# Windowed attention and a gated FFN on one core: the first fp32r term of each split unit's keys rounded on ScalarE and not on VectorE

## The chip, the cores and the metric

The kernel runs on one core of one Trainium2 chip. The metric is the device time of the whole program in microseconds (us). Three runs of the kernel before took 1072.38, 1073.99 and 1076.33 us, median 1073.99. One further execution, 1072.04 us, was profiled; all rows shown are from it.

## The reference

Sliding-window attention (each query sees itself and the 127 keys before it, with a linear bias per head), then a two-layer FFN with a sigmoid-gated unit on the attention's output, 4608 tokens of 512 features, all in float32:

```python
scores = scale * np.matmul(q, k.transpose(0, 1, 3, 2))       # q, k, v: (8, 8, 576, 64)
mask = (rel >= 0) & (rel < 128)                               # rel = query - key
scores = np.where(mask, scores + bias[None], -1000000000.0)
attn = np.exp(scores - np.max(scores, axis=-1, keepdims=True))
attn = attn / (np.sum(attn, axis=-1, keepdims=True) + 1e-09)
attn_out = np.matmul(attn, v)
x = attn_out.transpose(0, 2, 1, 3).reshape(4608, 512)
h = x @ w_in                                                  # 512 -> 2048
g = h * (1.0 / (1.0 + np.exp(-1.702 * h)))
return g @ w_out                                              # 2048 -> 512
```

## The kernel before

TensorE multiplies in fp32r, a float32 format with fewer mantissa bits. To keep float32 accuracy a number a is held as two fp32r terms: the first is a rounded, the second is a minus the first. A product then takes two or three matmuls.

The work has three parts in time. From the start to about 195 us attention of the first two batches runs in "whole" units, beside loads and the decoding of the weights. From about 195 to 765 us attention of batches 2 to 7 runs in 120 "split" units, woven into the FFN's steps. From 765 us to the end only the FFN is left, in a form that reuses precomputed combinations of the weights. The change touches only the middle part.

A split unit is one or two blocks of 128 queries of one pair of heads. Its steps, each a function of the kernel, go through the engines like this:

- `load`: queries `rq` and keys `rk` come by DMA on SP's queue. A unit has 256 or 128 queries (two blocks or one and a half, as columns) and 384 or 256 keys.
- `split_q` (L308): ScalarE copies `rq` into `Q`, the first term of the queries.
- `split_rest` (L326 to L328): VectorE copies `rk` into `K1`, the first term of the keys. GpSimd then subtracts to make the lower half of `Q` the second term (L327), and subtracts `K1` from `rk` to make `K2` (L328).
- `scores` (L350): TensorE multiplies `Q` with `K1` and `K2` into the PSUM tile `s_ps`.
- `biased` (L378): VectorE adds bias to `s_ps`, writes `pb` and its minimum `mins`.
- `exponents` (L397): ScalarE takes the exponential of `pb` with `mins` as its bias.
- `normal` (L408, L409, L422): VectorE makes the reciprocal of the sums and scales `pb` by it.
- `flip`, `high`, `low` (L458, L471, L477): TensorE transposes `pb` into `t_ps`; ScalarE rounds it to `ph`; VectorE subtracts to get `pl`.
- `mix` (L515) and `sum_up` (L545 to L554): TensorE multiplies with the values `VV`; ScalarE, GpSimd and VectorE add the halves into `xf`, the FFN's input.

Each call of `tick` issues these steps for several units at once: the keys and queries of unit n+1, the scores of unit n, the softmax of unit n-1, the transposes of n-2, the mix of n-3. `K1`, `K2` and `Q` have two buffers each, so `K1` of unit n+1 may be written only when the scores of unit n-1, which read the same buffer, are done.

Beside it an FFN step f runs 12 matmuls of 128x256 into `h_ps` (L577), then tanh on ScalarE (L582), the gate on VectorE (L583), the rounding `gh` on ScalarE (L586), the second term `gl` on GpSimd (L587), and 6 matmuls of 128x512 into `acc` (L597). `h_ps` has two buffers.

What sets the order within each engine is a scheduler that runs over the whole program when it is built: it plays the program through with durations of its own and writes each engine's instructions in the order that comes out. Each engine then executes its list strictly in order. A step that moves to another engine can so change the order on all engines.

Of the kernel before, what the change touches and what calls it, by code (L numbers as in the profile page):

```python
# [153 lines left out]
def tile_kernel(ctx: ExitStack, tc: tile.TileContext, q0, k0, v0, qT, kT, v, w_in, w_out, out):  # L154
    nc = tc.nc
# [164 lines left out]
    def split_rest(u):  # L320
        if u.whole:
            return
        u.K1 = att.tile([P, 3 * P], F32R, name="K1")
        u.K2 = att.tile([P, 3 * P], F32R, name="K2")
        Q, K1, K2, rq, rk = u.Q[:, :u.nq], u.K1[:, :u.nk], u.K2[:, :u.nk], u.rq[:, :u.nq], u.rk[:, :u.nk]
        nc.vector.tensor_copy(K1, rk)  # L326
        nc.gpsimd.tensor_tensor(Q[D:], rq[D:], Q[D:].bitcast(F32), ALU.subtract)  # L327
        nc.gpsimd.tensor_tensor(K2, rk, K1.bitcast(F32), ALU.subtract)  # L328

# [486 lines left out]
    def tick():  # L816

        nonlocal ticks
        n = ticks

        def stage(k, *steps):
            u = units[n + k] if 0 <= n + k < len(units) else None
            for step in steps:
                if u:
                    step(u)

        stage(1, split_q)
        stage(-2, flip, split_v)
        stage(0, load_v)
        stage(-1, biased)  # L830
        stage(1, split_rest)
        stage(-1, exponents)
        stage(-1, normal)
        stage(-2, high, low)
        stage(0, scores)
        stage(-3, mix)
        if n + 1 < len(units) and units[n + 1] and loads:
            load(loads.pop(0))
        for ct in full.get(n - 3, ()):
            if ct > seen + 1:  # L840
                send(ct)
        ticks += 1
# [29 lines left out]
    fetch_upto(1)  # L872
    split_q(units[0])
    split_rest(units[0])
    while ticks < due[0][0] + 3:
        tick()
# [161 lines left out]
```

## Time and profile before

| | us |
|---|---|
| median of three runs | 1073.99 |
| profiled execution, its own time | 1072.04 |
| its span, first to last instruction | 1070.3 |
| TensorE busy | 1041.9 (97%) |
| VectorE (DVE) busy | 756.6 (71%) |
| ScalarE (ACT) busy | 631.9 (59%) |
| GpSimd (POOL) busy | 625.9 (58%) |

The profiled execution's own time is 1.95 us below the median of the runs, and 1.7 us longer than its span. PE is TensorE's matmuls, PEld its weight loads, which overlap the matmuls. Ends of matmuls are modelled, so a busy PE is not proof that it does its work at its peak rate. In rows of instructions, "K<-rk" means that a tile K (K1 or K2; numbers are left out) is written from rk, and the figures behind the bar are the group's busy time in us and the mean duration of one in ns, then the idle time of the engine just before them. In rows of waits the figures are the total in us, the number of times and the longest. Timeline rows begin with the start and the duration in us; a bracket at the end is the engine's idle time before.

### The profile page before, as it was taken

The page shows a single profiled execution, that of the slowest core. Times are in us where ns is not written, and L with a number is a line of the kernel's source. Part 1 is how long each engine was busy: PE and PEld are TensorE (multiplying, and loading weights), DVE is VectorE, ACT ScalarE, POOL GpSimd, SP SyncE. Part 2 cuts the span into 40 slices and gives each one's busy share as a digit, 9 for nine tenths or more (in the row PEclk, how much of TensorE's full clock was granted, in tenths as well). Part 3 has the DMA queues.
Part 4 walks back from the last instruction along what each step waited for, and adds up shares of the span by engine and source line. Part 5 has one row for each costly group of instructions (what it writes and reads, how often), then busy time and mean ns, then how long its engine had stood idle before and what let it go on. Part 6 is the DMA issues. An engine that isn't in the chain of part 4 may idle for free.

```text
span 1070.3 us, 21638 instructions
## 1 busy us (share of the span) xinstructions
PE 1041.9 (97%) x6897; PEld 913.5 (85%) x6897; DVE 756.6 (71%) x2184; ACT 631.9 (59%) x1854; POOL 625.9 (58%) x831
## 2 busy tenths in 40 slices
PE   9979999999999999999999999999999999999998
PEld 5667877788989989899898989999898998998987
DVE  6896676379888897988888798888854345436343
ACT  6968775466766766566666756667543344335332
POOL 4677986367776776667677667767642233215121
PEclk9989999999999999999999999999999999999999
DMA  8983446223234224324323332342165456545541
GB/s 306 386 300 129 142 154 194 87 83 90 80 87 133 77 83 130 109 82 125 99 77 104 118 108 79 89 138 78 59 228 191 173 177 210 177 165 202 192 177 60
DMA packets 120274, 151.90 MB, mean 142 GB/s; under 512 B 40032, under 2 KB 96864, under 8 KB 120160
## 3 DMA queue, kind: packets, MB, share of 16 engines
q1 hardware_dynamic: 114400, 140.55, 41.1%
q10 hardware_dynamic: 5760, 9.96, 2.5%
q8 instruction: 55, 0.90, 0.3%
q14 instruction: 59, 0.48, 0.1%
HBM read 119.01 MB, written 31.46 MB: 141 GB/s over the span
## 4 chain that ended last, share of the span: by engine, by line
PE 68%; DVE 11%; ACT 3%; issue 3%; POOL 1%; DMA 1%; POOLq 0%; ACTq 0%; SPq 0%; DVEq 0%
PE acc L597 17%; PE h_ps L577 17%; PE accs L777 11%; PE X_ps L718 6%; PE Y_ps L718 4%; PE x_ps L515 4%; PE s_ps L350 4%; PE t_ps L458 3%; DVE pb L422 2%; ACT pb L397 1%; PE x_ps L492 1%; DVE K L326 1%; DVE pb L378 1%; DVE pl L477 1%; DVE xl L563 1%
## 5 line engine op out<-in xcount | busy, mean ns | idle before, releaser
L577 PE MATMUL h_ps<-xh,w 128*128 128x256 f32 x1536 | 256.8, 289 | 7.8 <-DVE g L583 6.6
L577 PEld LDWEIGHTS h_ps<-xh,w 128*128 128x128 f32 x1536 | 217.8, 190 | 28.4 <-issue 7.3
L597 PE MATMUL acc<-w,gh 128*128 128x512 f32 x768 | 222.6, 402 | 0.4
L587 POOL TENSOR_TENSOR gl<-g,gh 128x256 fp32r<-128x256 f32 x192 | 149.4, 779 | 113.6 <-ACT gh L586 81.9
L730 POOL TENSOR_TENSOR gs<-g,gs 128x512 fp32r<-128x512 f32 x48 | 63.5, 1322 | 169.9 <-PE Y_ps L718 120.4
L777 PE MATMUL accs<-w,gs 128*128 128x512 f32 x576 | 148.4, 393 | 0.3 <-POOL gs L730 0.3
L397 ACT ACTIVATE pb<-pb,mins 128x256 f32<-128x256 f32 (+2 forms) x216 | 104.9, 486 | 73.3 <-DVE mins L378 71.7
L597 PEld LDWEIGHTS acc<-w,gh 128*128 128x128 f32 x768 | 130.8, 189 | 18.3 <-ACT gh L586 1.0
L328 POOL TENSOR_TENSOR K<-rk,K 128x384 fp32r<-128x384 f32 (+1 forms) x120 | 108.9, 908 | 51.6 <-POOL Q L327 10.4
L577 PE MATMUL h_ps<-xl,w 128*128 128x256 f32 x768 | 134.5, 283 | 0.0
L597 PE MATMUL acc<-w,gl 128*128 128x512 f32 x384 | 128.0, 407 | 2.2 <-POOL gl L587 2.2
L586 ACT CAST gh<-g 128x256 fp32r<-128x256 f32 x192 | 77.2, 404 | 79.7 <-DVE g L583 74.4
L777 PEld LDWEIGHTS accs<-w,gs 128*128 128x128 f32 x576 | 102.2, 189 | 17.7 <-POOL gs L730 0.7
L577 PEld LDWEIGHTS h_ps<-xl,w 128*128 128x128 f32 x768 | 111.5, 189 | 4.1 <-issue 0.4
L422 DVE TENSOR_SCALAR pb<-pb,rec 128x256 f32<-128x256 f32 (+2 forms) x216 | 109.1, 541 | 3.3
L583 DVE SCALAR_TENSOR_TENSOR g<-g,h_ps 128x256 f32<-128x256 f32 x192 | 78.9, 412 | 39.4 <-ACT g L582 38.2
L582 ACT ACTIVATE g<-h_ps 128x256 f32<-128x256 f32 x192 | 72.7, 380 | 40.2 <-PE h_ps L577 29.7
L327 POOL TENSOR_TENSOR Q<-rq,Q 64x256 fp32r<-64x256 f32 (+1 forms) x120 | 83.5, 696 | 18.7 <-DVE pb L422 1.9
L378 DVE CUSTOM_DVE_ANT_0 pb<-s_ps,bias 128x256 f32<-128x256 f32 (+3 forms) x240 | 85.4, 376 | 1.2
L458 PE MATMUL t_ps<-ident,pb 128*128 128x128 f32 x408 | 80.6, 274 | 4.6 <-DVE pb L422 2.9
L408 DVE TENSOR_SCALAR rec<-sums 128x2 f32<-128x2 f32 (+3 forms) x144 | 43.8, 304 | 53.2 <-ACT pb L397 46.2
L477 DVE TENSOR_TENSOR pl<-t_ps,ph 128x512 fp32r<-128x512 f32 (+2 forms) x120 | 72.0, 601 | 3.2 <-ACT ph L471 3.0
(114 smaller groups left out, 2064.6 us busy)
## 6 DMA issues: line engine op xcount, KB each, us to landing
ring<-part SPq DMA_DIRECT2D x84, 512.0 KB, 3.2
rk<-kT SPq DMA_DIRECT2D x72, 192.0 KB, 2.5
rq<-qT SPq DMA_DIRECT2D x96, 128.0 KB, 2.2
out<-o ACTq DMA_DIRECT2D x34, 256.0 KB, 2.7
rw<-w_in SPq DMA_DIRECT2D x16, 512.0 KB, 6.6
rw<-w_out SPq DMA_DIRECT2D x16, 512.0 KB, 7.0
x<-xf SPq DMA_DIRECT2D x13, 512.0 KB, 3.2
xf<-x SPq DMA_DIRECT2D x13, 512.0 KB, 4.3
```

The source lines that it names most:

```text
L327: nc.gpsimd.tensor_tensor(Q[D:], rq[D:], Q[D:].bitcast(F32), ALU.subtract)
L328: nc.gpsimd.tensor_tensor(K2, rk, K1.bitcast(F32), ALU.subtract)
L378: nc.vector.tensor_tensor_reduce(b.p[ra:rb, cs:b.end], u.s[ra:rb, e, cs:b.end], bias[head][ra:rb, cs:b.end], -SCALE, BIG, ALU.add, ALU.min ...
L397: nc.scalar.activation(live, live, AF.Exp, bias=u.mins[:b.rows, e:e + 1], scale=-1.0, accum_out=u.sums[:b.rows, e:e + 1],)
L422: nc.vector.tensor_scalar(live, live, u.rec[:rows, e:e + 1], None, ALU.mult)
L458: nc.tensor.transpose(u.t[:c.n, w:w + b.rows], b.p[:b.rows, col:col + c.n], ident[:b.rows, :b.rows])
L477: nc.vector.tensor_tensor(u.pl[:m, a:z], u.t[:m, a:z], u.ph[:m, a:z].bitcast(F32), ALU.subtract)
L577: nc.tensor.matmul(h, w1[f][:, z, k * P:(k + 1) * P], x[:, k], start=(n == 0), stop=(n == len(ops) - 1))
L587: nc.gpsimd.tensor_tensor(gl, g, gh.bitcast(F32), ALU.subtract)
L597: products.append(nc.tensor.matmul(acc, g[:, t * P:(t + 1) * P], w2[f][:, z], start=(f == self.f0 and n == 0), stop=(f == self.f1 - 1 and ...
L718: nc.tensor.matmul(bank, w[:, z, k * P:(k + 1) * P], x[:, y, k], start=start and i == 0, stop=i == len(ops) - 1, skip_group_check=True)
L777: products.append(nc.tensor.matmul(self.acc[t], g[:, y, t * P:(t + 1) * P], w2[f][:, z], start=(f == 0 and n == 0), stop=(f == NF - 1 and ...
```

## The change

The copy that makes `K1` is issued to ScalarE and not to VectorE. It is the same copy, of the same shapes, 120 times.

```diff
         Q, K1, K2, rq, rk = u.Q[:, :u.nq], u.K1[:, :u.nk], u.K2[:, :u.nk], u.rq[:, :u.nq], u.rk[:, :u.nk]
-        nc.vector.tensor_copy(K1, rk)
+        nc.scalar.copy(K1, rk)
         nc.gpsimd.tensor_tensor(Q[D:], rq[D:], Q[D:].bitcast(F32), ALU.subtract)
         nc.gpsimd.tensor_tensor(K2, rk, K1.bitcast(F32), ALU.subtract)
```

The scheduler then writes other orders from the first split unit on. Up to there all engines' lists are the same, and the last part of the FFN differs only at its join with the middle part. Numbers at names tell the buffers' instances apart. In the following rows K1_6302, Q_6285 and the scores s_ps_6236 belong to the same ticks: s_ps_6236 reads the buffer (then called K1_6122) that K1_6302 writes next. Rows of L378 are called ISA here and CUSTOM_DVE_ANT_0 in the profile.

VectorE around this unit, before:

```order
L554 TENSOR_TENSOR xf_4797<-x_ps_6140,xb_6243 64x128
L326 CAST K1_6302<-rk_6075 128x384
L378 ISA pb_6298,mins_6297<-s_ps_6236,bias0_76 128x256
L378 ISA mins_6297 128x1
L378 ISA pb_6300,mins_6297<-s_ps_6236,bias0_76 128x256
L378 ISA mins_6297 128x1
L408 TENSOR_SCALAR rec_6310<-sums_6307 128x2
```

and VectorE at the same place now:

```order
L583 SCALAR_TENSOR_TENSOR g_6190<-g_6190,h_ps_6177 128x256
L477 TENSOR_TENSOR pl_6207<-t_ps_6205,ph_6206 128x384
L378 ISA pb_6298,mins_6297<-s_ps_6236,bias0_76 128x256
L378 ISA mins_6297 128x1
L378 ISA pb_6300,mins_6297<-s_ps_6236,bias0_76 128x256
L378 ISA mins_6297 128x1
L408 TENSOR_SCALAR rec_6310<-sums_6307 128x2
```

The cast stood directly ahead of the minima of the scores (it does so in 109 of the 120 units), and they now follow the subtractions of an earlier unit.

ScalarE around the same unit, before:

```order
L315 CAST VV_6292<-rv_6117 128x2x64
L582 ACTIVATE g_6272<-h_ps_6259 128x256
L586 CAST gh_6275<-g_6272 128x256
L308 CAST Q_6285<-rq_6074 128x256
L397 ACTIVATE pb_6298,sums_6307<-pb_6298,mins_6297 128x256
L397 ACTIVATE pb_6300,sums_6307<-pb_6300,mins_6297 128x256
```

and ScalarE now:

```order
L586 CAST gh_6193<-g_6190 128x256
L326 CAST K1_6302<-rk_6075 128x384
L308 CAST Q_6285<-rq_6074 128x256
L545 COPY xb_6243<-x_ps_6140 64x512
L315 CAST VV_6292<-rv_6117 128x2x64
L397 ACTIVATE pb_6298,sums_6307<-pb_6298,mins_6297 128x256
L397 ACTIVATE pb_6300,sums_6307<-pb_6300,mins_6297 128x256
L582 ACTIVATE g_6272<-h_ps_6259 128x256
L586 CAST gh_6275<-g_6272 128x256
```

The cast now stands directly ahead of Q's (so in 104 of the 120 units), the exponentials follow behind both, and here the tanh and the rounding of one FFN step have moved from ahead of them to behind them.

TensorE where this unit's pb is transposed, before:

```order
L597 MATMUL acc1_6019<-w2_5_776,gl_6276 128x512
L577 MATMUL h_ps_6416<-xh_5906,w1_7_957 128x256 x5
L577 MATMUL h_ps_6416<-xl_5907,w1_7_957 128x256 x4
L577 MATMUL h_ps_6496<-xh_5906,w1_8_1045 128x256
L458 MATMUL t_ps_6368<-ident_75,pb_6298 128x128 x2
L458 MATMUL t_ps_6368<-ident_75,pb_6300 128x128
L597 MATMUL acc0_6018<-w2_6_874,gh_6356 128x512
```

and TensorE now:

```order
L577 MATMUL h_ps_6416<-xh_5906,w1_7_957 128x256 x4
L458 MATMUL t_ps_6368<-ident_75,pb_6298 128x128 x2
L597 MATMUL acc0_6018<-w2_5_776,gh_6275 128x512
L597 MATMUL acc1_6019<-w2_5_776,gh_6275 128x512
L597 MATMUL acc0_6018<-w2_5_776,gh_6275 128x512
L597 MATMUL acc1_6019<-w2_5_776,gh_6275 128x512
L458 MATMUL t_ps_6368<-ident_75,pb_6300 128x128
```

The transposes of pb_6298 stand earlier among the matmuls of FFN step 7, and four matmuls of step 5, which stood ahead of both, now stand between them and the transpose of pb_6300. TensorE's instructions are the same in number and shape.

## The prediction

> **What bounds the kernel now.** I read the page first, for the engines' shares and how they lie over time.
>
> ```profile
> span 1070.3 us, 21638 instructions
> PE 1041.9 (97%) x6897; PEld 913.5 (85%) x6897; DVE 756.6 (71%) x2184; ACT 631.9 (59%) x1854; POOL 625.9 (58%) x831
> DVE  6896676379888897988888798888854345436343
> ACT  6968775466766766566666756667543344335332
> ```
>
> TensorE is busy for 97% of the span, so it is the bound as a whole. DVE runs at eight to nine tenths in the middle slices, ACT at five to seven tenths. The next view was the busy time in three stretches: ahead of the split units, with them, behind them. After the stretch's length stand PE, PEld, DVE, ACT and POOL, each with its count.
>
> ```profile
> 0.00:195.00 195.00, 181.07 (x1151) 136.23 (x1152) 141.61 (x372) 143.60 (x428) 137.90 (x138) 0.97 0.67 225
> 195.00:765.00 570.00, 561.72 (x3882) 509.17 (x3881) 476.79 (x1588) 368.05 (x1159) 394.60 (x612) 1.00 0.33 97
> 765.00:1070.30 305.30, 299.10 (x1868) 268.11 (x1866) 138.24 (x225) 120.24 (x269) 93.40 (x82) 1.00 0.50 172
> ```
>
> Only the middle stretch holds the changed casts. There PE is busy for 561.72 of 570 us: 8.28 us of idle time is all that the rows offer to be won. DVE stands at 476.79/570 = 84%, ACT at 368.05/570 = 65%. So the question is not how much work moves, but whom TensorE waits for. The waits in this stretch, first PE's, then those of its weight loads, answer that:
>
> ```profile
> PE t_ps L458 <- DVE pb L422: 2.9, 5, 1.2
> PE s_ps L350 <- DVE mins L378: 1.8, 2, 1.2
> PE t_ps L458 <- DVE pl L477: 1.5, 1, 1.5
> PE acc L597 <- POOL gl L587: 1.2, 1, 1.2
> PE h_ps L577 <- DVE xh L561: 0.4, 1, 0.4
> PE x_ps L515 <- DVE xf L554: 0.2, 1, 0.2
> ```
>
> ```profile
> PEld t_ps L458 <- DVE pb L422: 4.2, 7, 1.4
> PEld acc L597 <- POOL gl L587: 1.6, 1, 1.6
> PEld acc L597 <- ACT gh L586: 0.7, 2, 0.3
> PEld x_ps L492 <- ACT pw L443: 0.3, 1, 0.3
> PEld x_ps L515 <- ACT ph L471: 0.2, 1, 0.2
> PEld x_ps L515 <- ACT g L582: 0.2, 1, 0.2
> ```
>
> PE's own waits come to 8.0 us, and 6.8 of them (2.9 + 1.8 + 1.5 + 0.4 + 0.2) end with a DVE instruction. ACT ends none of PE's and 1.4 us of the weight loads'. The scaled pb that comes too late for its transposes is the largest: 4.2 us in 7 waits by the weight loads' row. Each number is small: 0.5% of the median, about what a measurement of this kernel can tell from no change, is 5.4 us.
>
> **The work that moves.** The groups, with shapes kept apart:
>
> ```profile
> L326 DVE CAST K<-rk 128x384 fp32r<-128x384 f32 x72 | 34.3, 477 | 6.9 <-PE s_ps L350 4.3 <-issue 1.9 <-PE t_ps L435 0.2
> L326 DVE CAST K<-rk 128x256 fp32r<-128x256 f32 x48 | 18.8, 391 | 3.7 <-PE t_ps L435 2.1 <-PE s_ps L350 1.3
> L308 ACT CAST Q<-rq 128x256 fp32r<-128x256 f32 x96 | 38.9, 405 | 14.4 <-PE s_ps L350 10.3 <-issue 1.9 <-POOL VV L316 1.1
> L729 ACT CAST gs<-g 128x512 fp32r<-128x512 f32 x48 | 29.9, 623 | 18.9 <-DVE g L725 18.9
> ```
>
> DVE loses 34.3 + 18.8 = 53.1 us, 0.443 a unit: from 84% to 423.7/570 = 74%. On ACT the same copy of 256 columns takes 405 ns (Q's cast); 384 columns have no row, and half way between 405 and 623 is 514 ns. ACT so gains 48 x 0.405 + 72 x 0.514 = 56.4 us, 0.470 a unit: from 65% to 424.5/570 = 74%. The two engines come out level, and neither becomes the fullest: that stays PE. The edit issues no DMA of its own; on ACT's queue the casts now stand ahead of some issues of `out<-o`, which nothing in the middle waits for, and on SP's queue the scheduler only changed places among loads, which no PE row waits for.
>
> What a cast really occupied on DVE depends on its neighbour. The group's least, median and greatest duration, then two casts in the timeline, with what GpSimd did:
>
> ```profile
> L326 DVE CAST K<-rk x120: 275/353/1000, 202.5 to 763.9; 128x384 fp32r<-128x384 f32 x72, 128x256 fp32r<-128x256 f32 x48
> ```
>
> ```profile
> 401.64 0.74 POOL L587 TENSOR_TENSOR gl<-g,gh 128x256 fp32r<-128x256 f32 x1
> 401.98 0.62 DVE L326 CAST K<-rk 128x384 fp32r<-128x384 f32 x1
> 402.52 0.41 DVE L378 CUSTOM_DVE_ANT_0 pb<-s_ps,bias 128x256 f32<-128x256 f32 x1
> 402.97 0.51 ACT L397 ACTIVATE pb<-pb,mins 128x256 f32<-128x256 f32 x1 [1.17 <-DVE mins L378]
> ...
> 410.85 0.29 DVE L326 CAST K<-rk 128x256 fp32r<-128x256 f32 x1 [0.40 <-PE s_ps L350]
> 411.28 0.74 POOL L328 TENSOR_TENSOR K<-rk,K 128x256 fp32r<-128x256 f32 x1 [0.60 <-PE s_ps L350]
> ```
>
> The cast at 401.98 began while GpSimd worked on gl and ended at 402.60, after gl's end at 402.38; the narrower one at 410.85, with GpSimd idle, took 0.29. So part of the 53.1 us is waiting beside GpSimd. Q's cast on ACT has a mean of 405 ns for 256 columns, whatever GpSimd does.
>
> Here a rule speaks against the change. The Trainium skill, Perfetto Trace Analysis, section Optimizing Scalar/DVE Operations, says that where an operation has a VectorE performance mode VectorE is the faster engine, and that work is worth moving to ScalarE if VectorE is saturated. The trace agrees in direction for an undisturbed cast (0.29 against 0.405 us) but hardly for the means (391 against 405 ns). By that rule, with DVE unsaturated at 84%, the move would cost the difference, 56.4 - 53.1 = 3.3 us if all of it lay on the path, and give 1073.99 + 3.3 = 1077.3.
>
> **Where it stood and where it stands.** In the order of before the cast stands directly ahead of the minima in 109 of 120 units: DVE does K1, then the minima that ScalarE's exponentials need. The rows above show one such chain: cast, minimum at 402.52, exponential at 402.97 after 1.17 us in which ACT idled. Now the cast stands on ACT ahead of Q's cast. The waits of ACT, DVE and POOL in the stretch:
>
> ```profile
> ACT pb L397 <- DVE mins L378: 70.6, 80, 3.1
> ACT Q L308 <- PE s_ps L350: 12.4, 22, 1.2
> DVE rec L408 <- ACT pb L397: 45.1, 70, 1.5
> DVE g L583 <- ACT g L582: 15.7, 18, 5.1
> DVE K L326 <- PE s_ps L350: 5.6, 11, 1.0
> POOL K L328 <- DVE K L326: 4.2, 4, 1.8
> ```
>
> ACT idles ahead of an exponential 80 times, 70.6/80 = 0.88 us on average. That is the hole into which 0.47 us of cast falls. The minima come 0.44 us sooner; ACT is free 0.88 - 0.47 = 0.41 us sooner than the minima came before. So in these 80 units the exponentials start about 0.41 us earlier, although ACT does more. In the other 40 there was no hole, and ACT's queue is 0.47 us longer at most.
>
> **The sum, on the profiled execution's 1072.04 us.**
> 1. Transposes that wait for pb (4.2 us, 7 times): 7 x 0.41 = 2.9 us less, at best; by DVE's lighter load alone, 53.1/476.8 = 11% of 4.2, it is 0.5. I take -2.0, nearer the first, since the cast stood in that very chain.
> 2. Scores that wait for the minima to free s_ps (1.8 us, twice): 2 x 0.44 = 0.9 at best, 0.2 at least. I take -0.7.
> 3. pl and the DVE rest (1.5 + 0.4 + 0.2 us, three waits): between 0.2 and 3 x 0.44 = 1.3. I take -0.3, near the low end, since they stand behind other DVE work.
> 4. ACT's longer queue: in the 40 units without a hole pb comes 0.47 later. Now 7 of 120 transposes wait, so 40 x 7/120 x 0.47 = 1.1; by load alone 56.4/368 = 15% of the 1.4 us of weight loads that ACT ends, 0.2. I take +0.8. The ceiling, all 40 on the path, is 18.8.
> 5. The cast's own wait for the scores before last (DVE 5.6 us, 11 times): it goes to ACT, where Q's cast already waits for the same event (12.4 us, 22 times), and now ends ahead of Q's. No new wait, 0. K2 on GpSimd follows K1 as before; it waited 4.2 us for it and no row of PE waits for K2, since the scores that need it come a tick later: 0 between 0 and 4.2. If that cover were gone, the scores would be late next.
> 6. The orders that the scheduler rewrote: TensorE has the same instructions, and all that can change is its waits. From none left to twice as many, that is -8.3 to +8.3. I take 0, with +-3 for the range: a third of the idle time.
> 7. The stretches ahead and behind (195 + 305.3 us): same work, same order but for the join: 0.
>
> Sum: -2.0 - 0.7 - 0.3 + 0.8 = -2.2, so 1069.8 for a run like the profiled one. The median of the runs was 1.95 us above it; so the forecast for a median is 1071.8 us.
>
> **The rivals.**
> A larger gain. DVE's waits vanish wholly: 6.8 us, less the 0.8 of step 4, is -6.0, or 1068.0; all idle time, 8.3, gives 1065.7. For it: DVE ends 85% of what PE waits for. Against it: waits on pb have other causes on DVE too, and one that goes uncovers the next (POOL's gl, 1.2 to 1.6 us).
> Slower. ACT is served in order, and the cast waits on ACT for the scores; tanh and gh of an FFN step behind it wait along, so gh and with it TensorE's acc matmuls come late. It is at the 40 units without a hole, 0.47 us each. If half reach PE, that is +9.4 - 3.0 = +6.4, or 1080.4; if all, 1073.99 + 18.8 - 3.0 = 1089.8. It decides (5.4 us slower) from (5.4 + 3.0)/0.47 = 18 of the 40 units on. For it: DVE's gate waited 15.7 us for tanh in 18 waits, and the reciprocal 45.1 us in 70 for exponentials, so ACT is already the late one there. Against it: PE's waits name ACT nowhere. The Trainium skill, Perfetto Trace Analysis, section Tensor Engine Instruction, calls the queues of ScalarE, VectorE and GpSimd strict FIFO; the 22 waits at Q's cast agree, as ACT did nothing else in them.
> That the change does not do what it says can't be: the order shows the cast on ACT 120 times.
>
> **Chances and range.** Forecast 0.55, with its own range of 1068.6 to 1076; the larger gain 0.27; slower 0.18. The forecast and the steps' ends lie within 0.5% of 1073.99, that is between 1068.6 and 1079.4. The larger gain counts as faster. The range for 8 in 10 runs from 1063 (all idle time and some stretched matmuls that the modelled ends hide) to 1081 (just past the point at which half of the 40 units reach PE).
>
> **What would show it.** Right: DVE falls to 420 to 430 us in the stretch and ACT rises to 420 to 430; the 128x384 cast takes about 0.51 us on ACT; ACT's wait for minima falls from 70.6 to under 45; PE's idle time in the stretch falls from 8.3 to about 6, with less under t_ps <- pb. Wrong: PE or its weight loads wait on ACT's gh, ph or g for more than 3 us; or the scores wait for K on POOL; or PE's idle time rises. The steps most in doubt are the fourth and the sixth.

## The result and the profile after

The changed kernel took 1069.21 us (median of 15 runs, 1063.64 to 1072.32), the kernel before in the same comparison 1076.59 us (15 runs, 1071.88 to 1081.04). The ratio is 0.9926, with a 95% interval of 0.9902 to 0.9949: faster by 0.74%, inside the predicted range. The median lies inside the forecast's own range of 1068.6 to 1076 too, but that is luck: the kernel before was 2.6 us slower in this comparison than the 1073.99 us that the forecast started from. The ratio applied to 1073.99 gives 1066.0, past that range, between the 1068.0 and 1065.7 of the rival "a larger gain".

The profiled execution, however, has the same span as that of before. From the page of the changed kernel:

```profile
span 1070.3 us, 21658 instructions
PE 1045.2 (98%) x6897; PEld 916.1 (86%) x6897; DVE 713.1 (67%) x2064; ACT 674.6 (63%) x1974; POOL 622.8 (58%) x831
```

The reason lies ahead of the change. The first 100 us, whose order is the same in both kernels, busy time by engine, before and then after; the column behind POOL is the granted TensorE clock:

```profile
0.00:50.00 50.00, 44.90 (x283) 29.51 (x283) 36.85 (x140) 39.65 (x120) 25.50 (x34) 0.97 0.96 343
50.00:100.00 50.00, 42.51 (x276) 32.54 (x274) 42.30 (x88) 38.13 (x120) 39.16 (x37) 0.93 0.67 230
```

```profile
0.00:50.00 50.00, 45.45 (x271) 29.07 (x272) 34.34 (x137) 37.52 (x113) 22.70 (x33) 0.93 0.95 333
50.00:100.00 50.00, 41.05 (x249) 30.48 (x249) 41.92 (x77) 35.16 (x109) 38.24 (x34) 0.86 0.67 220
```

This execution was granted 0.93 and 0.86 of the clock, that of before 0.97 and 0.93, and fewer matmuls started. Over all profiled executions of this document the first cast of Q comes at 191.1 to 191.8 us where 0.93 was granted from 50 to 100 us, and at 194.8 to 198.2 us where it was 0.86 to 0.89; kernels with the casts on VectorE and with casts on ScalarE are in both groups. So whole spans of single executions don't compare; the part between two fixed instructions does. I take the middle part from the first cast of Q (L308) to the first matmul of the last part (L718, X_ps). Before:

```profile
L308 ACT CAST Q<-rq x120: 288/405/419, 191.1 to 762.9; 128x256 fp32r<-128x256 f32 x96, 128x128 fp32r<-128x128 f32 x24
L718 PE MATMUL X_ps<-xB,ring x288: 277/283/386, 789.5 to 1058.0; 128*128 128x256 f32 x144
```

After:

```profile
L308 ACT CAST Q<-rq x120: 292/402/418, 197.6 to 763.2; 128x256 fp32r<-128x256 f32 x96, 128x128 fp32r<-128x128 f32 x24
L718 PE MATMUL X_ps<-xB,ring x288: 274/283/386, 788.0 to 1057.2; 128*128 128x256 f32 x144
```

The part took 789.5 - 191.1 = 598.4 us before and 788.0 - 197.6 = 590.4 us after: 8.0 us less, which is 0.74% of 1076.6. The head took 6.5 us longer (197.6 against 191.1) and the rest 1.5 us longer, and the three cancel in the span.

The stretch from 195 to 765 us of the changed kernel, then TensorE's waits in it:

```profile
195.00:765.00 570.00, 566.55 (x3929) 514.95 (x3930) 440.67 (x1486) 415.34 (x1299) 393.94 (x618) 1.00 0.34 99
```

```profile
PE h_ps L577 <- DVE g L583: 1.0, 2, 0.5
PE t_ps L458 <- DVE pb L422: 0.9, 2, 0.6
PE s_ps L350 <- DVE mins L378: 0.8, 2, 0.4
PE t_ps L458 <- DVE pl L477: 0.5, 2, 0.3
PE h_ps L577 <- DVE xl L563: 0.4, 1, 0.4
```

PE's idle time fell from 8.28 to 570 - 566.55 = 3.45 us, and 47 more matmuls lie in the same 570 us (3929 against 3882): the part gained more than its idle time lost. A matmul's modelled end hides the beginning of each stall; the run with the old order, below, shows how much. DVE stands at 77%, ACT at 73%. The other engines' waits, and the cast itself:

```profile
ACT pb L397 <- DVE mins L378: 24.0, 30, 3.6
ACT K L326 <- PE s_ps L350: 8.8, 15, 1.6
DVE rec L408 <- ACT pb L397: 55.4, 69, 1.8
POOL K L328 <- ACT K L326: 35.4, 51, 2.7
```

```profile
L326 ACT CAST K<-rk x120: 400/510/526, 209.3 to 763.6; 128x384 fp32r<-128x384 f32 x72, 128x256 fp32r<-128x256 f32 x48
```

ACT waits for minima 30 times and not 80. The cast is steady on ACT; none takes long beside GpSimd.

### The profile page after: what moved, and what is told of

The parts are those of the page before. It is cut to its first block, busy times and chain, and to the rows that moved or that the text cites. A ratio compares the mean times of both kernels' runs of the same rounds, so it can differ in the third digit from the quotient of the medians.

```text
span 1070.3 us, 21658 instructions
## 1 busy us (share of the span) xinstructions
PE 1045.2 (98%) x6897; PEld 916.1 (86%) x6897; DVE 713.1 (67%) x2064; ACT 674.6 (63%) x1974; POOL 622.8 (58%) x831
## 5 line engine op out<-in xcount | busy, mean ns | idle before, releaser
L577 PE MATMUL h_ps<-xh,w 128*128 128x256 f32 x1536 | 254.2, 288 | 8.7 <-DVE g L583 8.1
L577 PEld LDWEIGHTS h_ps<-xh,w 128*128 128x128 f32 x1536 | 215.6, 189 | 30.0 <-issue 8.5
L597 PE MATMUL acc<-w,gh 128*128 128x512 f32 x768 | 219.8, 401 | 0.1
L597 PEld LDWEIGHTS acc<-w,gh 128*128 128x128 f32 x768 | 131.4, 189 | 18.5 <-ACT gh L586 0.5
L577 PE MATMUL h_ps<-xl,w 128*128 128x256 f32 x768 | 139.6, 286 | 0.4 <-DVE xl L563 0.4
L328 POOL TENSOR_TENSOR K<-rk,K 128x384 fp32r<-128x384 f32 (+1 forms) x120 | 109.6, 914 | 42.5 <-ACT K L326 35.4
L577 PEld LDWEIGHTS h_ps<-xl,w 128*128 128x128 f32 x768 | 113.8, 190 | 5.5 <-DVE xl L563 0.6
L422 DVE TENSOR_SCALAR pb<-pb,rec 128x256 f32<-128x256 f32 (+2 forms) x216 | 101.9, 507 | 3.2
L378 DVE CUSTOM_DVE_ANT_0 pb<-s_ps,bias 128x256 f32<-128x256 f32 (+3 forms) x240 | 86.0, 378 | 10.6 <-PE s_ps L350 8.2
L408 DVE TENSOR_SCALAR rec<-sums 128x2 f32<-128x2 f32 (+3 forms) x144 | 44.6, 310 | 62.5 <-ACT pb L397 55.8
```

The lines of the kernel that those rows point to most:

```text
L378: nc.vector.tensor_tensor_reduce(b.p[ra:rb, cs:b.end], u.s[ra:rb, e, cs:b.end], bias[head][ra:rb, cs:b.end], -SCALE, BIG, ALU.add, ALU.min ...
L422: nc.vector.tensor_scalar(live, live, u.rec[:rows, e:e + 1], None, ALU.mult)
L577: nc.tensor.matmul(h, w1[f][:, z, k * P:(k + 1) * P], x[:, k], start=(n == 0), stop=(n == len(ops) - 1))
L597: products.append(nc.tensor.matmul(acc, g[:, t * P:(t + 1) * P], w2[f][:, z], start=(f == self.f0 and n == 0), stop=(f == self.f1 - 1 and ...
```

## The experiments

Three theories stood at first: *work* (VectorE is rid of the casts), *place* (only that they stood ahead of the minima) and *order* (the scheduler's new order of everything). To hold an order fixed, some kernels write it out: a list per engine, and between neighbours on it an edge that sets the order of issue and waits for nothing.

**The changed kernel again.** No edit.

> The changed kernel once more, beside the kernel before on the same chip, as the measure for the three others. Three theories of the gain of 0.7 to 0.8%: (work) VectorE no longer does the cast, and all that stood behind it there comes sooner; (place) it matters only that the cast stood ahead of the minima on VectorE; (order) the scheduler's new order on TensorE and the other engines brings it, whichever engine casts. All expect a ratio of 0.990 to 0.995. If a new profile has a slow head again (first Q cast at 197 us), the middle part, from there to the first X_ps matmul, should still be 590 us, against 598 before.

```profile
L308 ACT CAST Q<-rq x120: 293/402/418, 195.4 to 759.8; 128x256 fp32r<-128x256 f32 x96, 128x128 fp32r<-128x128 f32 x24
L718 PE MATMUL X_ps<-xB,ring x288: 274/283/386, 784.6 to 1053.6; 128*128 128x256 f32 x144
```

Ratio 0.9930 (0.9902 to 0.9958); middle part 784.6 - 195.4 = 589.2 us. The result and its place in the program repeat. Two executions of this one kernel differ by 1.2 us in the middle part, so no difference of that size between two profiles is read as an effect.

**The old order, casts on ScalarE.**

```diff
-        nc.vector.tensor_copy(K1, rk)
+        nc.scalar.copy(K1, rk)
...
+    written_order(nc, tc)    # all engines as before; each cast where ScalarE was when it began on VectorE
```

> The casts run on ScalarE, but every other instruction of every engine stands in the order of the kernel before, written out and enforced; each cast stands on ScalarE ahead of the instruction that began there next after the cast had begun on VectorE. Work: nearly the whole gain, ratio 0.990 to 0.995. Place: the same. Order: no gain, 0.998 to 1.002, or a loss if ScalarE's longer queue now makes waits that the scheduler could not plan for.

```profile
L308 ACT CAST Q<-rq x120: 287/406/420, 198.2 to 762.3; 128x256 fp32r<-128x256 f32 x96, 128x128 fp32r<-128x128 f32 x24
L718 PE MATMUL X_ps<-xB,ring x288: 277/283/386, 788.5 to 1057.6; 128*128 128x256 f32 x144
```

Ratio 0.9897 (0.9870 to 0.9923); middle part 590.3 us, as with the new order. The new order is not needed for the gain. TensorE's waits in the stretch:

```profile
PE t_ps L458 <- DVE pb L422: 1.2, 1, 1.2
PE acc L597 <- POOL gl L587: 0.7, 1, 0.7
PE h_ps L577 <- POOL xl L563: 0.4, 1, 0.4
PE s_ps L350 <- DVE mins L378: 0.2, 1, 0.2
```

TensorE's matmuls come in the same order here as in the kernel before, so the time from each start to the next can be compared pair by pair in the two traces. From the first split scores to the last part 8.0 us were saved: 3.7 us ahead of the transposes (`t_ps`), 2.1 us ahead of the scores (`s_ps`), and 2.2 us ahead of `h_ps`, `acc` and `x_ps` together. Ten stalls, which all show as waits in the kernel before, account for 6.8 us of it. The longest, transposes that waited for `pl`, showed 1.49 us of idle time and gave back 1.65 us; the 0.16 us between lay under the modelled end of the matmul before. (The same comparison of the two executions of the changed kernel gives differences of up to 0.8 us for one kind of matmul.)

**The new order, casts on VectorE.**

```diff
+    written_order(nc, tc)    # all engines as changed; each cast on VectorE ahead of what followed it before
```

> The reverse: every engine keeps the order of the changed kernel, but the casts run on VectorE, each directly ahead of the instruction that followed it there before. Work and place: the gain is lost, ratio 0.998 to 1.004. Order: the gain stays, 0.990 to 0.995.

```profile
L308 ACT CAST Q<-rq x120: 292/405/417, 194.8 to 770.2; 128x256 fp32r<-128x256 f32 x96, 128x128 fp32r<-128x128 f32 x24
L718 PE MATMUL X_ps<-xB,ring x288: 274/283/387, 794.7 to 1064.0; 128*128 128x256 f32 x144
```

Ratio 1.0010 (0.9988 to 1.0032); middle part 599.9 us. With the new order alone nothing is gained. The two runs together settle it: the order theory falls.

**Casts on VectorE, behind the minima.** The old order, but in 109 units the cast stands directly behind the minima that followed it.

```diff
-L326 CAST K1_6302<-rk_6075 128x384
 L378 ISA pb_6298,mins_6297<-s_ps_6236,bias0_76 128x256
 L378 ISA mins_6297 128x1
 L378 ISA pb_6300,mins_6297<-s_ps_6236,bias0_76 128x256
 L378 ISA mins_6297 128x1
+L326 CAST K1_6302<-rk_6075 128x384
```

> The order of the kernel before on all engines, casts on VectorE, but in the 109 units in which the cast stood directly ahead of the minima it now stands directly behind them. Place: most of the gain without moving any work, 0.991 to 0.996. Work: little, 0.997 to 1.001, since VectorE still does all casts and the reciprocal and the scaling stand behind them. Order: none, 0.998 to 1.002.

```profile
L308 ACT CAST Q<-rq x120: 289/405/418, 191.5 to 761.0; 128x256 fp32r<-128x256 f32 x96, 128x128 fp32r<-128x128 f32 x24
L718 PE MATMUL X_ps<-xB,ring x288: 277/283/387, 787.5 to 1056.7; 128*128 128x256 f32 x144
```

Ratio 0.9968 (0.9945 to 0.9991), between what the two theories expected; middle part 596.0 us, 2.4 less than before. Place is worth something, by the profiles about a third of the gain (by the ratios 0.0032 of 0.0074), and not "most of it". TensorE's list is again that of before: compared start by start, the transposes and the scores gained 4.4 us and `acc` 0.5, while `h_ps` and `x_ps` lost 2.5 (TensorE waits 1.4 us for xh and 1.0 for xf there, 0.4 and 0.2 before).

**Half of the casts.** The old order; units with odd numbers cast on ScalarE.

```diff
-        nc.vector.tensor_copy(K1, rk)
+        (nc.scalar.copy if u.at % 2 else nc.vector.tensor_copy)(K1, rk)
```

> Every second cast on ScalarE, the others on VectorE; all orders as in the kernel before, the moved casts where they stood in the run with all of them on ScalarE. If each cast that leaves VectorE brings its share, half of the gain: 0.994 to 0.997, and a middle part of about 594 us between 598 and 590. If a threshold of VectorE's load decides, the whole gain or none.

```profile
L308 ACT CAST Q<-rq x120: 287/404/418, 191.2 to 756.9; 128x256 fp32r<-128x256 f32 x96, 128x128 fp32r<-128x128 f32 x24
L718 PE MATMUL X_ps<-xB,ring x288: 277/283/386, 783.1 to 1051.6; 128*128 128x256 f32 x144
```

Ratio 0.9916 (0.9881 to 0.9950); middle part 591.9 us. Half the casts brought 6.5 of the 8.1 us that all bring in the old order. That is more than the half that was expected, 0.994 to 0.997 and about 594 us; the first work that leaves VectorE seems to be worth more than the next, though the interval does not exclude an equal share, and only the units with odd numbers were tried.

**The casts twice.** The old order, casts on VectorE, and again on ScalarE into K2, which GpSimd then overwrites.

```diff
         nc.vector.tensor_copy(K1, rk)
+        nc.scalar.copy(K2, rk)
```

> The kernel before in its own order, casts on VectorE, and besides the same 120 casts again on ScalarE at the places of the run with the old order; their result goes into K2, which GpSimd then overwrites. ScalarE has the load of the changed kernel, and VectorE keeps its own. It measures the fourth step of the prediction, the price of ScalarE's longer queue, forecast at +0.8 us between 0.2 and 18.8. Work theory with a free ScalarE: 0.999 to 1.002. If ScalarE's time costs about as much as VectorE's: 1.006 to 1.010, and the gain would be the difference of two large terms.

```profile
195.00:765.00 570.00, 562.83 (x3876) 509.20 (x3876) 467.19 (x1580) 409.68 (x1281) 390.71 (x606) 1.00 0.33 97
```

```profile
L308 ACT CAST Q<-rq x120: 289/404/421, 197.2 to 771.0; 128x256 fp32r<-128x256 f32 x96, 128x128 fp32r<-128x128 f32 x24
L719 PE MATMUL X_ps<-xB,ring x288: 277/283/386, 797.1 to 1066.1; 128*128 128x256 f32 x144
```

Ratio 0.9996 (0.9967 to 1.0024); middle part 599.9 us. ACT works 409.68 us here and not 368.05, and that costs 1.5 us by the profiles, about as much as two executions of one kernel differ, and nothing by the ratio. ScalarE's added time was all but free.

**Casts on GpSimd.** In the order that the scheduler makes.

```diff
-        nc.vector.tensor_copy(K1, rk)
+        nc.gpsimd.tensor_copy(K1, rk)
```

> The casts on GpSimd instead of VectorE or ScalarE, in the order that the scheduler then makes. If all that counts is that VectorE is rid of them, the gain is the changed kernel's, 0.990 to 0.996. If GpSimd, at 69% of the middle part, then is late with gl and K2, or its longer work holds up VectorE's copies beside it, 0.998 to 1.010.

```profile
L308 ACT CAST Q<-rq x120: 292/405/417, 196.1 to 768.0; 128x256 fp32r<-128x256 f32 x96, 128x128 fp32r<-128x128 f32 x24
L718 PE MATMUL X_ps<-xB,ring x288: 277/283/387, 795.8 to 1064.3; 128*128 128x256 f32 x144
```

```profile
L422 DVE TENSOR_SCALAR pb<-pb,rec 128x256 f32<-128x256 f32 x168 | 98.5, 609 | 3.4
L326 POOL CAST K<-rk 128x384 fp32r<-128x384 f32 x72 | 37.4, 519 | 16.3 <-PE s_ps L350 9.2 <-issue 4.1 <-POOL Q L327 1.3
L326 POOL CAST K<-rk 128x256 fp32r<-128x256 f32 x48 | 20.0, 417 | 16.8 <-PE s_ps L350 14.5 <-issue 1.3 <-PE t_ps L435 0.7
```

The scalings in the changed kernel:

```profile
L422 DVE TENSOR_SCALAR pb<-pb,rec 128x256 f32<-128x256 f32 x168 | 81.5, 508 | 2.5
```

Ratio 0.9982 (0.9959 to 1.0005); middle part 599.7 us. VectorE is rid of the casts here too, and nothing is gained. What it costs in exchange: GpSimd stood still for 23.7 us for the scores that release K1, with gl behind it, and VectorE's scalings of 256 columns took 609 ns each, against 508 in the changed kernel and 552 before. Over the middle part VectorE's busy time fell by 24.8 us only (470.6 against 495.4). How these two share the loss is not separated.

**A read in the cast's place.** As with the old order and casts on ScalarE, but in 109 units VectorE takes the maximum of 256 score columns in PSUM, unused, where the cast stood.

```diff
+        if ...:    # in 109 units
+            nc.vector.tensor_reduce(
+                att.tile([P, 1], F32, name="scr", bufs=1), u.s[:, :len(u.blocks), P:], mybir.AxisListType.XY, ALU.max)
```

> As the run with the old order and all casts on ScalarE, but in 109 units VectorE reads 256 columns of the scores in PSUM into one column of maxima that nobody uses, at the place where the cast stood. So VectorE has about its old load, and its old start of the minima, but no copy between SBUF tiles beside GpSimd. If VectorE's time is what the change gave back: the gain is gone, 0.997 to 1.002, middle part 596 to 600 us. If it was the copies' waiting beside GpSimd, in both directions: most of the gain stays, 0.989 to 0.994.

```profile
L374 DVE TENSOR_REDUCE scr<-s_ps 128x1 f32<-128x256 f32 x89 | 37.2, 419 | 8.9 <-PE s_ps L350 8.0
L374 DVE TENSOR_REDUCE scr<-s_ps 128x1 f32<-128x128 f32 x20 | 5.6, 278 | 0.4 <-PE s_ps L350 0.3
```

```profile
L308 ACT CAST Q<-rq x120: 288/405/420, 191.8 to 759.0; 128x256 fp32r<-128x256 f32 x96, 128x128 fp32r<-128x128 f32 x24
L721 PE MATMUL X_ps<-xB,ring x288: 277/283/387, 785.1 to 1054.1; 128*128 128x256 f32 x144
```

Ratio 0.9956 (0.9934 to 0.9979); middle part 593.3 us, between 590.3 without the read and 598.4. The 37.2 + 5.6 = 42.8 us of reads took back 3.0 us by the profiles, and 0.0059 of the ratio, 6.3 us, by the runs. Neither theory's number came out. Of the two the 3.0 us is the better measure: three runs with a middle part of 589.2 to 590.4 us have ratios from 0.9897 to 0.9930, a spread of 3.5 us within their intervals, and the 6.3 us start from the lowest of the three.

**A cast that does not wait for GpSimd.** The plain copy's waiting beside GpSimd is another candidate. The old order, casts on VectorE, in 89 units as a two-input operation that takes the scores times zero from PSUM.

```diff
-            nc.vector.tensor_copy(K1, rk)
+            nc.vector.scalar_tensor_tensor(K1, s, 0.0, rk, ALU.mult, ALU.add)
```

> The order of the kernel before on all engines, casts on VectorE in their old places; but in 89 units the cast is a two-input operation with the scores in PSUM as its other input, 0 times the scores plus the keys, which rounds the keys as before. By the rows of L583 and L477 it should take about 0.41 us for 256 columns and 0.55 us for 384, whatever GpSimd does, against means of 0.39 and 0.48 with single casts up to 1.0 us before: some 5 us more of VectorE's time in all. If VectorE's time is what counts: no gain or a loss, 1.000 to 1.004, middle part 598 to 602 us. If the plain copy's waiting beside GpSimd is what made the casts dear: a gain although VectorE works longer, 0.993 to 0.998, middle part 592 to 596 us.

```profile
L330 DVE SCALAR_TENSOR_TENSOR K<-s_ps,rk x89: 406/427/559, 219.2 to 763.9; 128x256 fp32r<-128x256 f32 x45, 128x384 fp32r<-128x384 f32 x44
```

```profile
L308 ACT CAST Q<-rq x120: 290/406/418, 191.7 to 762.9; 128x256 fp32r<-128x256 f32 x96, 128x128 fp32r<-128x128 f32 x24
L728 PE MATMUL X_ps<-xB,ring x288: 277/283/387, 789.5 to 1058.3; 128*128 128x256 f32 x144
```

None of these 89 casts exceeds 0.56 us, where copies went up to 1.0; yet the ratio is 1.0004 (0.9979 to 1.0030) and the middle part 597.8 us. But the new form takes longer than a copy beside an idle GpSimd (a mean of 0.42 us for 256 columns, against the 0.29 at 410.85), 31 plain copies are left, and VectorE's busy time over the middle part stayed the same, 494.9 against 495.4 us. So evening out the long casts gains nothing while VectorE's time stays; whether copies that are short because they never wait would gain is not shown.

**Other work off VectorE: 96 of the 216 scalings.** The kernel before, casts on VectorE, but each second block's scaling on ScalarE, in the order that the scheduler makes.

```diff
-            nc.vector.tensor_scalar(live, live, u.rec[:rows, e:e + 1], None, ALU.mult)
+            if e:
+                nc.scalar.activation(live, live, AF.Copy, scale=u.rec[:rows, e:e + 1])
+            else:
+                nc.vector.tensor_scalar(live, live, u.rec[:rows, e:e + 1], None, ALU.mult)
```

> The kernel before, casts on VectorE, but the scaling of each two-block unit's second block on ScalarE (96 of 216; 50 us off VectorE, about as much as the casts). If any work that leaves VectorE's queue helps alike: 0.990 to 0.995, a middle part near 590 us. If the casts' place ahead of the minima made them dearer than other work: a smaller gain, 0.995 to 0.999.

```profile
L308 ACT CAST Q<-rq x120: 284/406/418, 191.3 to 754.0; 128x256 fp32r<-128x256 f32 x96, 128x128 fp32r<-128x128 f32 x24
L721 PE MATMUL X_ps<-xB,ring x288: 274/283/387, 779.2 to 1048.5; 128*128 128x256 f32 x144
```

Ratio 0.9927 (0.9897 to 0.9956); middle part 587.9 us. Some 50 us of quite other work, moved from VectorE to ScalarE, gains at least as much as the casts (10.5 us by the profiles): the gain does not need the casts or their place. What this run's own order brings was not measured apart.

**Both: casts and 96 of the 216 scalings on ScalarE.**

> The changed kernel, and further the scaling of each two-block unit's second block moves from VectorE to ScalarE (96 of 216, about 50 us more off VectorE and 49 onto ScalarE: 68% and 82% of the middle part). If VectorE's queue is still what TensorE waits for, a further gain: 0.986 to 0.991. If ScalarE is now the late one, the gain goes back: 0.993 to 1.000.

```profile
195.00:765.00 570.00, 569.52 (x3974) 520.48 (x3974) 403.84 (x1412) 458.24 (x1411) 396.26 (x622) 1.00 0.34 99
```

```profile
L308 ACT CAST Q<-rq x120: 283/402/419, 197.2 to 755.3; 128x256 fp32r<-128x256 f32 x96, 128x128 fp32r<-128x128 f32 x24
L721 PE MATMUL X_ps<-xB,ring x288: 277/283/386, 780.8 to 1049.7; 128*128 128x256 f32 x144
```

Ratio 0.9852 (0.9813 to 0.9891), median 1062.31 us; middle part 583.6 us, PE idle for 570 - 569.52 = 0.48 us of the stretch. The two moves together gain 598.4 - 583.6 = 14.8 us, less than the 8.0 + 10.5 = 18.5 us of each alone. This version beats both kernels.

**Casts and all scalings on ScalarE.** The two-way choice above becomes ScalarE for every block.

> The changed kernel with all 216 scalings on ScalarE: ScalarE at about 91% of the middle part, VectorE at about 60%. If ScalarE's queue then is what TensorE waits for, the gain turns: slower than with half the scalings (0.985), 0.990 to 1.010. If VectorE's queue is all that counts: 0.978 to 0.985.

```profile
195.00:765.00 570.00, 567.00 (x3943) 517.29 (x3943) 353.54 (x1279) 488.91 (x1516) 393.24 (x620) 1.00 0.34 99
```

```profile
L308 ACT CAST Q<-rq x120: 294/405/420, 197.8 to 760.7; 128x256 fp32r<-128x256 f32 x96, 128x128 fp32r<-128x128 f32 x24
L718 PE MATMUL X_ps<-xB,ring x288: 277/283/386, 786.3 to 1055.4; 128*128 128x256 f32 x144
```

Ratio 0.9901 (0.9871 to 0.9931); middle part 588.5 us. The intervals of this version and the last overlap, but the middle part is 4.9 us longer. With VectorE at 62% and ScalarE at 86% part of the gain is given back: VectorE's gate now waits 52.9 us for ScalarE's tanh, 33.3 in the version with 96 scalings moved, and TensorE 2.1 us for the gate, 0.5 there. By now ScalarE's time has its price.

## Why the prediction was right or wrong

The direction, the range and most of the mechanism held; the size did not. The sum said -2.2 us for the middle, the profiles say -8.0.

- *The bound.* TensorE waits for VectorE, as read. But "8.28 us of idle time is all that the rows offer to be won" was wrong as a limit. The version with 96 scalings moved too gained 14.8 us. PE's busy rows hold stalls, since the ends of matmuls are modelled; 3882 matmuls in the stretch became 3974. PE's idle time fell to 3.45 us, not to "about 6".
- *The work that moves.* 0.51 us for 384 columns held (mean 513 ns). The casts did come off VectorE and onto ScalarE, but the stretch's busy times, 440.67 and 415.34, are not the forecast 420 to 430 on either side. Instructions that follow each other on an engine overlap in the trace (the cast at 401.98 ends at 402.60, the next began at 402.52), so the 53.1 and 56.4 us of the groups need not be what an engine's busy time changes by. Over the whole middle part, the same work in both, VectorE fell from 495.4 to 450.8 us and ScalarE rose from 383.7 to 425.4: 44.6 us less and 41.7 more.
- *The hole on ACT.* ACT's wait for minima fell further than forecast, from 70.6 to 24.0 us against "under 45".
- *Steps 1 to 3*, together -3.0 us, hold the terms that were mis-sized. The visible waits in the changed kernel went about as forecast (t_ps for pb from 2.9 to 0.9 us, s_ps for minima from 1.8 to 0.8). The stalls behind them are longer than the rows show. With TensorE's old list and the casts on ScalarE, the starts give -2.1 us for the transposes that waited for pb, against -2.0 in step 1; -2.1 for the scores, against -0.7 in step 2; -2.5 for pl, xh and xf, against -0.3 in step 3; and -1.3 for the rest, which these steps don't count. The error lies in the price of one mean cast, at most 0.44 us, for each late event: the ten stalls gave back 0.30 to 1.65 us each. Lateness can add up over several casts. Ahead of the longest stall, that for pl, VectorE worked from 622.98 to 632.57 us without a pause above 0.2 us, and two casts, of 0.97 and 0.35 us, lay in that run; what each of them cost there is not shown apart. In the changed kernel TensorE's list is another, so its 8.0 us can't be split pair by pair. Place alone, the chain that step 1 describes, measured 2.4 us.
- *Step 4* (+0.8) held: the casts' load added to ScalarE cost nothing by the ratio and 1.5 us by the profiles. The slower rival did not appear here; the gate that waits for tanh, which it names, shows its price when all scalings move.
- *Step 5* (0): ACT's wait for the scores is 8.8 us at K's cast and 0.7 at Q's, no more than the 12.4 at Q's before. GpSimd waits 35.4 us for K1 where it waited 4.2, but all its idle time ahead of K2 fell, from 51.6 to 42.5 us, and TensorE never waits for K2: the cover named there held.
- *Step 6* (0, +-3) held: the order with the casts held on VectorE gave 599.9 against 598.4 us, and with them held on ScalarE 590.4 against 590.3.
- *The rule against the change.* The Trainium skill's advice in Perfetto Trace Analysis, section Optimizing Scalar/DVE Operations, to move work if VectorE is saturated, would have kept the cast where it was, at 84%, and gives 1077.3. The measurement decides: at 84% the move paid, and at 77% the next one paid again.
- *The rivals.* The larger gain came about, by the waits on VectorE that it names; its limit, the idle time in the rows, was too low.

What stays open is whether VectorE's time is all of it. Over the middle part VectorE is busy for 495.4 us before, 450.8 with the casts on ScalarE in the old order, and 477.2 with the reads in their place. The reads so put back 26.4 of 44.6 us, which in proportion is 4.8 of the 8.1 us; 3.0 came. The difference of 1.8 us is little more than two executions of one kernel differ by. It may come from K1 no longer passing through VectorE's queue on its way to GpSimd and TensorE; no run separates that.

## What to carry to other kernels

Where an engine feeds the bound one through a queue that is served in order, its time has a price well below saturation: here some 50 us off VectorE at 84%, put on a ScalarE at 65%, gave 8 to 10.5 us, and on a GpSimd at 69% nothing. Don't take the bound engine's idle time for the limit of a gain when its busy time is modelled; measure the stretch between two fixed instructions, and where the bound engine's list stays the same compare its starts pair by pair. Price a late event by all the work that moves out of the unbroken run ahead of it, not by one instruction. And when a scheduler reorders everything, hold the order and move the work, then the reverse: two runs tell which of the two it was.

## What the runs showed of the hardware

The same head of the program took 191.1 us in one execution and 197.6 us in another, with clocks of 0.97 and 0.93 against 0.93 and 0.86 granted in its first two 50 us; 6.5 us, nearly as much as the effect under study. The traces don't show which of the two, the lower clock or the fewer matmuls, came first. And a plain VectorE copy that took 0.62 and up to 1.0 us beside GpSimd and 0.29 with GpSimd idle could be replaced in 89 units by a form that never exceeds 0.56 us without any gain in the total (1.0004), while VectorE's busy time stayed the same (494.9 against 495.4 us): evening out the long copies was worth nothing by itself.
